# Putting the tail of the output product into the other arm of the range check's branch

## The chip, the cores and the metric

One core of a Trainium2 chip. The metric is the device time of one execution in microseconds (us), median of several; a few hundredths of a per cent matter here, so most readings are taken from the start times in the trace, which hold nanoseconds. PE is TensorE, PEld its weight loads, DVE is VectorE, ACT is ScalarE, POOL is GpSimd, SP is SyncE. A q behind an engine's name means its sequencer. "Product" means one matmul instruction; the operand that is loaded ahead of it is its weights, and it writes a PSUM tile, which VectorE's additions read. A run within 1.5% of the fastest run of its kernel is called fast.

## The reference

Attention of 8 x 32 queries over the last 2048 positions of a cache, 32 query heads on 4 key heads, with the projections ahead and behind:

```python
def reference(x, k_cache, v_cache, wq, wo):
    B, Sq, D = x.shape                      # 8, 32, 1024
    Hq, Dh = 32, 128
    Hkv, Sk = k_cache.shape[1], k_cache.shape[2]   # 4, 8192
    W = min(4096, max(256, Sk // 4))        # 2048
    ...
    scores = jnp.einsum("bhqd,bhkd->bhqk", q, k) * (Dh ** -0.5)
    p = _softmax(scores, axis=-1)
    o = jnp.einsum("bhqk,bhkd->bhqd", p, v)
    return (lambda x, *d: x.transpose(*d))(o, 0, 2, 1, 3).reshape(B, Sq, Hq * Dh) @ wo
```

## The kernel before

The kernel takes the exponentials without subtracting the row maximum, which is right while every row's sum stays in a range. It checks that range at the end, counts the rows that pass with a product against a column of ones, takes the minimum, and branches: if any row failed, an exact fallback runs instead (it never runs on this data). Every engine loads the flag into a register and branches. `hint_branch` puts a branch hint that names the fallback on PE's sequencer, 4.9 us ahead of the branch.

```python
            with tc.manual_schedule(engines=order):
                fast.run()
            hint_branch(tc, (E.PE,))
            with tc.manual_schedule(engines=order):
                flagi = fast.tail_begin()
        safe = nc.values_load(flagi[0:1, 0:1], min_val=0, max_val=1)

        with tc.If(safe < 1, label="fallback"):          # L78
            ...                                          # exact attention, exact output product
            out_proj(tc, wo, OT_e, out_flat, fast, ...)  # leaves state so that the tail gives the same result

        with tc.manual_schedule(engines=order):
            fast.tail_end()
```

The tail is the output product of the last key head for the last 128 rows. It has four column groups of 512, 256, 128 and 128 columns. Each group is eight products into one PSUM tile (a piece is two of them), one addition on VectorE and one output DMA. Before the change the 512-column group is issued ahead of the branch and everything else behind it:

```python
    def o_pieces(self, g, t, cuts=(512, 512)):
        ...
            if i == 0:
                st["ps"] = self.open_ps = self.ps_m.tile([P, 512], FP32, name="op_ps", tag="m")   # two buffers
            ps = st["ps"]
            for k in range(i * 2, i * 2 + 2) if mm is not False else ():
                nc.tensor.matmul(ps[:, 0:w], lhsT=self.OT[...], rhs=self.wo_t[gq][:, c, n0:n0 + w], ...)   # L293
            if i == 3 and mm is not True:
                ...
                    nc.vector.tensor_tensor(out=o_t[:, 0:w], in0=ps[:, 0:w], in1=acc, op=ALU.add)          # L303
                    eng = nc.sync if n0 in (0, 768) else nc.scalar
                    eng.dma_start(out=self.out[t * P:(t + 1) * P, n0:n0 + w], in_=o_t[:, 0:w])             # L305

    def tail_begin(self):
        self.pv_last()
        for p in self.after[:-2]:
            p()
        flagi = self.check_all()
        for p in self.after[-2:]:
            p()
        self.last = self.o_pieces(self.Hkv - 1, 1, (512, 256, 128, 128))
        for p in self.last[:3]:
            p()
        self.last[3](mm=True)
        return flagi

    def tail_end(self):
        self.last[3](mm=False)
        for p in self.last[4:]:
            p()

    def check_all(self):
        ...
        nc.tensor.matmul(cnt[0:1, 0:2 * ncol], lhsT=self.ones_c[:, :], rhs=self.ok[:, :, :], start=True, stop=True)   # L524, the count product
        low = ck.tile([1, 1], FP32, name="low")
        nc.vector.tensor_reduce(out=low[:, :], in_=cnt[0:1, 0:2 * ncol], op=ALU.min, axis=AX.X)                       # L526
        flagi = ck.tile([1, 1], I32, name="flagi")
        nc.vector.tensor_scalar(out=flagi[:, :], in0=low[:, :], scalar1=float(P) - 0.5, scalar2=None, op0=ALU.is_ge)  # L528
        return flagi
```

## Time and profile before

| | before |
|---|---|
| median of the first 3 runs | 187.18 us (186.95 to 484.08) |
| profiled run | 186.85 us, span 185.0 us, granted clock 1.0 |
| PE busy | 179.5 us, 97% of the span |
| start of the count product | 177.09 us |
| start of the last addition | 182.34 us |
| last output DMA issued / waited for by SP | 182.66 / 184.16 us |

The 484.08 us is the first of the runs and was not looked into. The distance from the start of the count product to the start of the last addition is called **the tail** from here on. Taken from the trace in nanoseconds it is 5.256 us. Everything the change touches lies in it.

In the timeline of the profile a line reads: start in us, length in us, engine, source line, operation, output tile <- input tiles, shapes, number of instructions merged, and in brackets how long the engine was idle before and what is thought to have ended that. First PE's products and then its weight loads, kernel before:

```profile
177.09 0.22 PE L524 MATMUL cnt_ps<-ok,ones_c 128*1 128x128 bf16 x1
177.24 2.76 PE L293 MATMUL op_ps<-wo_sb,OT 128*128 128x512 bf16 x12
180.15 2.15 PE L293 MATMUL op_ps<-wo_sb,OT 128*128 128x256 bf16 x24
...
177.96 1.54 PEld L293 LDWEIGHTS <-OT 128*128 128x128 bf16 x8 [0.19 <-DVE OT L422]
180.12 1.39 PEld L293 LDWEIGHTS <-OT 128*128 128x128 bf16 x17 [0.61 <-DVEq L78]
181.70 0.43 PEld L293 LDWEIGHTS <-OT 128*128 128x128 bf16 x7 [0.19 <-issue]
```

The second PE line is twelve products of 512 columns ahead of the branch, the third the 24 narrow ones behind it. Within a group the starts follow each other in 0.216 us (512 columns), 0.108 (256) and 0.056 (128); a product that keeps this distance is called in step. Across the branch they do not: the last product ahead of it starts at 179.620 and the next at 180.149, 0.529 later. 0.313 us are lost. The weight-load lines show both places where PE stood still: ahead of 180.12, and ahead of 181.70.

The events of the branch line on the sequencers of VectorE and PE, kernel before (operation, count, duration in ns min/median/max, start):

```profile
L78 DVEq COMPARE_BRANCH  x1: 72/72/72, 178.9 to 178.9; - x1
L78 PEldq COMPARE_BRANCH  x1: 249/249/249, 178.9 to 178.9; - x1
L78 DVEq EVENT_SEMAPHORE  x1: 21/21/21, 179.5 to 179.5; - x1
L78 PEldq EVENT_SEMAPHORE  x1: 51/51/51, 180.0 to 180.0; - x1
```

PE's sequencer runs ahead of its products: it branches at 178.9 while products issued earlier run until 180.0. But in the arm that is taken it then has a semaphore step, and that step happens only at 180.0. The arm is empty in the source. The build fills it, and as I read it because the fallback raises semaphores that the empty arm does not: an engine waits until its own count is complete and adds the difference. The label "DVEq L78" in the weight-load line names VectorE's step, which was long done at 179.5.

The VectorE lines of the same stretch, kernel before:

```profile
177.84 0.24 DVE L526 TENSOR_REDUCE low<-cnt_ps 1x1 f32<-1x128 f32 x1
178.11 0.14 DVE L528 TENSOR_SCALAR flagi<-low 1x1 int32<-1x1 f32 x1
180.04 0.69 DVE L303 TENSOR_TENSOR o_t<-op_ps,oacc 128x512 bf16<-128x512 f32 x1 [1.03 <-PE op_ps L293]
181.22 0.74 DVE L303 TENSOR_TENSOR o_t<-op_ps,oacc 128x256 bf16<-128x256 f32 x2 [0.49 <-PE op_ps L293]
182.34 0.29 DVE L303 TENSOR_TENSOR o_t<-op_ps,oacc 128x128 bf16<-128x128 f32 x1 [0.38 <-PE op_ps L293]
```

The fourth line merges two additions: the 256-column one (181.220 to 181.645) and the first 128-column one. The last group writes the PSUM buffer that the 256-column addition reads, and its first product starts at 181.697, right behind that addition's end; in step it would have been 181.466. That is a second loss of 0.231 us. The chain that ended last holds this wait (start, length, what):

```profile
181.22 0.43 DVE o_t L303
181.66 0.04 issue
181.70 0.62 PE op_ps L293 x8
```

### The profile page before, as it was taken

To read this page: it belongs to the slowest core of one execution; us is meant where nothing else is said; L and a number is where in the kernel's file an instruction comes from. 1 tells how busy PE (TensorE), PEld (TensorE's weight loads), DVE (VectorE), ACT (ScalarE), POOL (GpSimd) and SP (SyncE) were. 2 spreads that over 40 slices of the span, in tenths; PEclk is the share of its full clock that TensorE was granted. 3 is DMA by queue.
4 is the path that set the end of the run, shared out by engine and by line. 5 is a ranking of instruction groups with operands and counts; after the bars stand their busy time and mean duration, and the time that the engine had idled before them with its cause. 6 is when DMAs were issued, how large, how long until landed. Compare 5 with 4: busy or idle time off the path is not lost. (4 is left out here: it accounts for less than half of the span.)

```text
span 185.0 us, 5079 instructions
## 1 busy us (share of the span) xinstructions
PE 179.5 (97%) x2056; PEld 153.7 (83%) x2072; DVE 115.4 (62%) x268; ACT 131.8 (71%) x133; POOL 94.7 (51%) x150
## 2 busy tenths in 40 slices
PE   7999999999999999999999999999999999999993
PEld 2889999999999999987878999987777888888743
DVE  0138799994586685586467558647745855355372
ACT  2207899786789787878787677787877888888700
POOL 2000008949939959929944980796299289600000
PEclk9999999999999999999999999999999999999999
DMA  5999999998999999999999999999999999980012
GB/s 151 324 391 415 413 414 396 198 231 278 346 332 297 305 329 337 412 215 244 363 357 244 362 386 252 186 342 397 249 381 320 228 288 246 299 131 0 4 58 62
DMA packets 53082, 51.73 MB, mean 280 GB/s; under 512 B 39744, under 2 KB 40256, under 8 KB 53056
## 3 DMA queue, kind: packets, MB, share of 16 engines
q1 hardware_dynamic: 52480, 50.90, 97.8%
q10 hardware_dynamic: 576, 0.49, 0.8%
q8 instruction: 16, 0.26, 0.6%
q14 instruction: 10, 0.08, 0.1%
HBM read 41.42 MB, written 0.52 MB: 227 GB/s over the span
## 5 line engine op out<-in xcount | busy, mean ns | idle before, releaser
L469 ACT ACTIVATE pT<-s_ps 128x1024 bf16<-128x1024 f32 x128 | 128.9, 1025 | 33.3 <-PE s_ps L467 32.3
L259 POOL TENSOR_SCALAR kTv<-kb 32x512 bf16<-32x512 bf16 x140 | 93.7, 670 | 65.1 <-DMA k_raw<-in_k_cache_dram 26.7
L478 PEld LDWEIGHTS <-pT 128*128 128x128 bf16 x1024 | 68.5, 98 | 3.1
L467 PEld LDWEIGHTS <-kT 128*128 128x128 bf16 x368 | 34.8, 98 | 10.3
L293 PE MATMUL op_ps<-wo_sb,OT 128*128 128x512 bf16 (+2 forms) x128 | 33.0, 353 | 0.8
L273 PE MATMUL q_ps<-xT,wq_sb 128*128 128x256 bf16 x192 | 28.1, 273 | 0.0
L478 PE MATMUL o_ps<-va_112,pT 128*128 128x129 bf16 x352 | 27.1, 220 | 0.0
L478 PE MATMUL o_ps<-va_113,pT 128*128 128x129 bf16 x352 | 27.0, 220 | 0.1
L478 PE MATMUL o_ps<-va_114,pT 128*128 128x129 bf16 x320 | 24.7, 220 | 0.0
L249 DVE STREAM_TRANSPOSE kb<-k_raw 128x512 bf16<-128x512 bf16 x36 | 23.8, 684 | 0.0
L415 DVE RECIPROCAL RL_all<-o_ps 128x2 f32<-128x2 f32 x32 | 5.3, 164 | 27.5 <-PE o_ps L478 27.5
L420 DVE TENSOR_SCALAR o_sb<-o_ps,RL_all 128x128 bf16<-128x128 f32 x64 | 19.5, 346 | 1.1
L467 PEld LDWEIGHTS <-kTv 128*128 128x128 bf16 x144 | 13.9, 98 | 5.1
L273 PEld LDWEIGHTS <-wq_sb 128*128 128x128 bf16 x192 | 17.0, 98 | 1.2
L467 PE MATMUL s_ps<-QT_63,kT 128*128 128x256 bf16 x112 | 16.8, 273 | 0.0
L422 DVE STREAM_TRANSPOSE OT<-o_sb 128x256 bf16<-128x256 bf16 x32 | 14.3, 446 | 1.1
L467 PE MATMUL s_ps<-QT_66,kT 128*128 128x256 bf16 x96 | 14.4, 273 | 0.1
L293 PEld LDWEIGHTS <-OT 128*128 128x128 bf16 x144 | 11.3, 98 | 2.9 <-DVEq L78 0.6
L467 PE MATMUL s_ps<-QT_65,kT 128*128 128x256 bf16 x80 | 12.0, 273 | 0.1
L467 PE MATMUL s_ps<-QT_64,kT 128*128 128x256 bf16 x80 | 12.0, 272 | 0.1
L300 DVE TENSOR_TENSOR oacc<-op_ps,oacc 128x512 f32<-128x512 f32 x8 | 5.5, 683 | 7.4 <-PE op_ps L293 7.4
L409 DVE COPY va_113<-v_sb 128x2048 bf16<-128x2048 bf16 x11 | 9.5, 861 | 0.0
(46 smaller groups left out, 105.2 us busy)
## 6 DMA issues: line engine op xcount, KB each, us to landing
v_sb<-in_v_cache_dram SPq DMA_DIRECT2D x29, 512.0 KB, 6.8
wo_sb<-in_wo_dram SPq DMA_DIRECT2D x16, 512.0 KB, 6.8
wq_sb<-in_wq_dram SPq DMA_DIRECT2D x14, 512.0 KB, 7.4
k_raw<-in_k_cache_dram SPq DMA_DIRECT2D x13, 512.0 KB, 6.5
v_sb<-in_v_cache_dram SPq DMA_DIRECT2D x6, 256.0 KB, 5.8
wq_sb<-in_wq_dram SPq DMA_DIRECT2D x4, 256.0 KB, 6.4
kT<-in_k_cache_dram SPq DMA_TRANSPOSE x36, 6.6
k_raw<-in_k_cache_dram SPq DMA_DIRECT2D x2, 256.0 KB, 7.7
```

Of the source, the lines that this page charges most:

```text
L249: nc.vector.transpose(out=st["kb"][:, sl, :], in_=self.k_raw[ui][:, sl, :])
L259: nc.gpsimd.tensor_scalar(out=out, in0=in_, scalar1=1.0, scalar2=1.0, op0=ALU.mult, op1=ALU.mult)
L273: nc.tensor.matmul(st["ps"][:, 0:self.NQ], lhsT=self.wq_t[g, i][:, c % (DC // 2), hl * P:(hl + 1) * P], rhs=self.xT[:, c, :], start=(c == ...
L293: nc.tensor.matmul(ps[:, 0:w], lhsT=self.OT[:, gq, c, t * P:(t + 1) * P], rhs=self.wo_t[gq][:, c, n0:n0 + w], start=(k == 0), stop=(k == 7))
L300: nc.vector.tensor_tensor(out=acc, in0=ps[:, 0:w], in1=acc, op=ALU.add)
L409: self.nc.vector.tensor_copy(out=self.va[ui % 3][:, :, 0:self.Dh], in_=self.v_sb[ui][:, :, :])
L415: nc.vector.reciprocal(out=rl[:, ui * QT_N:(ui + 1) * QT_N], in_=o_ps[:, :, Dh])
L420: nc.vector.tensor_scalar(out=o_sb[:, qt, :, :], in0=o_ps[:, qt, 0:Dh].rearrange("p (i c) -> p c i", c=4), scalar1=rl[:, ui * QT_N + qt:ui ...
L422: nc.vector.transpose(out=self.OT[:, g * QT_N:(g + 1) * QT_N, :, b * self.Sq:(b + 1) * self.Sq], in_=o_sb[:, :, :, :])
L467: nc.tensor.matmul(s_ps[:, jj, :], lhsT=self.kT[ui][:, c * CJ + jj, :], rhs=q_u, start=True, stop=True)
L469: nc.scalar.activation(out=pT[:, :, :], in_=s_ps[:, :, :], func=ACT.Exp, bias=0.0, scale=self.scale)
L478: nc.tensor.matmul(o_ps[:, qt, 0:self.VW], lhsT=pT[:, jj, qt * P:(qt + 1) * P], rhs=va[:, j, 0:self.VW], start=(j == 0 and qt == 0), stop= ...
```

## The change

The intent: no wait at the branch. The tail becomes the other arm, so that the arm taken is not empty; the integer minimum is loaded directly, without a compare to a flag; the load stands eight products (four pieces) ahead of the branch; and the two 128-column groups take PSUM banks of another pool. That pool now lives longer, so the fallback gets by with less PSUM (its edits never run here, so no run shows that they are right).

```diff
@@ the branch
-                flagi = fast.tail_begin()
-        safe = nc.values_load(flagi[0:1, 0:1], min_val=0, max_val=1)
-
-        with tc.If(safe < 1, label="fallback"):
+                low = fast.tail_begin()
+                safe = nc.values_load(low[0:1, 0:1], min_val=0, max_val=P)
+                fast.tail_mid()
+
+        with tc.If(safe < P, label="fallback") as arms:
...
-        with tc.manual_schedule(engines=order):
-            fast.tail_end()
+        with arms.Else():
+            with tc.manual_schedule(engines=order):
+                fast.tail_end()
@@ pools
+        self.ps_o = pool("ps_o", 2, long_ctx, space=PSUM)
...
-        self.ps_o = pool("ps_o", 2, space=PSUM)
@@ o_pieces: the PSUM tile of a group may be handed in, in a dictionary st (parameter and call cut)
-            if i == 0:
-                st["ps"] = self.open_ps = self.ps_m.tile([P, 512], FP32, name="op_ps", tag="m")
-            ps = st["ps"]
+            if i == 0 and n0 not in st:
+                st[n0] = self.ps_m.tile([P, 512], FP32, name="op_ps", tag="m")
+            ps = st[n0]
@@ tail_begin (its lines self.open = {} and low = self.check_all() cut), tail_mid, tail_end
-        for p in self.last[:3]:
+        for p in self.last[:2]:
             p()
+        return low
+
+    def tail_mid(self):
+        self.last[2]()
         self.last[3](mm=True)
-        return flagi
+        for p in self.last[4:6]:
+            p()
+        for n0 in (768, 896):
+            self.open[n0] = self.ps_o.tile([self.P, 512], FP32, name="op_ps", tag="o_ps")
 
     def tail_end(self):
         self.last[3](mm=False)
-        for p in self.last[4:]:
+        for p in self.last[6:]:
             p()
@@ check_all
-        low = ck.tile([1, 1], FP32, name="low")
+        low = ck.tile([1, 1], I32, name="low")
         nc.vector.tensor_reduce(out=low[:, :], in_=cnt[0:1, 0:2 * ncol], op=ALU.min, axis=AX.X)
-        flagi = ck.tile([1, 1], I32, name="flagi")
-        nc.vector.tensor_scalar(out=flagi[:, :], in0=low[:, :], scalar1=float(P) - 0.5, scalar2=None, op0=ALU.is_ge)
-        return flagi
+        return low
@@ the fallback: scores copied to SBUF in pieces, the lines that prepared the shared tail removed (cut)
```

## The prediction

> **What bounds it now.** The page's first part has PE busy 97% of 185.0 us. Up to about 177 us the change alters no instruction's order on any engine. What counts is the tail, read from the timeline of the last 8 us: one 128x512 product every 0.216 us, the last one ahead of the branch starting at 179.62 and ending at 180.0. The chain that ended last then holds only PE products and VectorE additions, 180.15 to 182.63. The last output DMA is issued at 182.66, lands 1.5 us later, and 0.8 us of closing barriers follow.
>
> **What the tail loses before.** Two PE bubbles:
> 1. Branch, 0.31 us. The flag (142 ns on VectorE, after the 236 ns minimum) is ready at 178.25; PE's sequencer loads it from 178.29 to 178.78 and branches at 178.95 (0.25 us), while products queued ahead keep PE going. But the empty arm evens out semaphore counts: there PE's sequencer waits for PE's own last product (its step is at 180.04). The next product starts at 180.149 instead of 179.62+0.216=179.836. (PE's weight load shows 0.6 us idle, released by VectorE at L78; VectorE's step there was done by 179.55, so that label is not the cause.)
> 2. Buffer, 0.23 us. The last 128-column group reuses the PSUM buffer of the 256-column group and waits for its addition (ends 181.645): first product 181.697 instead of 181.410+0.056.
>
> **What the change does.** It removes the flag's compare, loads the integer minimum directly, eight products before the branch (four of 512, four of 256 columns), makes the tail the other arm (no self-wait of PE ahead of it), and gives the two 128-column groups the other pool's PSUM banks. The fallback's edits do not run.
>
> Walk: minimum ends 178.07, load about 178.11 to 178.60. Products queued ahead last until 178.97: no bubble expected, some 0.2 us to spare. Without the compare, the preceding 512-column addition ends near 178.8 instead of 179.0, so the 256 group's buffer is free in time. Branch about 179.2 to 179.45; the first product behind it is due at 179.836+4x0.108=180.27. The other engines need 0.46 to 0.59 us from branch start to their next instruction; even that fits. The Trainium skill ("Runtime: NRT & Kernel Launch", Instruction fetch mechanics) says that a taken branch outside the loaded window stalls for a fetch; the trace of before shows PE's own delay only as under 1.1 us. PE keeps its hint.
>
> So: last 256 product starts 180.59, addition 180.90 to 181.33; 128 groups back to back, additions from 181.35 and 181.80. The last addition started at 182.34 before: 0.54 us earlier. Landing and barriers follow unchanged; up to 0.1 may be lost as the last output DMAs come closer together. ScalarE gains a counting step behind its last issue, off the path.
>
> **Predicted.** 187.18 is the median of three with one outlier; the other runs are near 186.9. Saving about 0.5 us (0.3%): **186.6 us**, 8 in 10 between 186.1 and 187.2. Faster by over 2%: 0.01; within 2%: 0.98; slower: 0.01.
>
> **Right if** after shows no PE gap over 0.1 us between the count product and the last product; 256-column products every 0.108 us across the branch; the last group starting about 181.15 without waiting for VectorE; the last addition near 181.8; span near 184.5. **Wrong if** PE stalls at the earlier load (gap before the 512 products behind it) or behind the branch (fetch of the arm), or the last DMA takes longer to land.
>
> **What would make it wrong.** A 0.3 us stall of PE at load or branch cancels half; an arm on a page that is not loaded could cost 1 us; run-to-run scatter is about as large as the gain.

## More of the kernel before

The trace has PE's step as a wait for and a raise of one semaphore, 103, which PE's own products raise; the last of them raised it at 180.014, and the step starts at 180.042. So on PE the step waits for PE's own last product.

## The result, and the profile after

| | before | after |
|---|---|---|
| median | 186.95 us (186.69 to 484.08, 6 runs) | 186.38 us (185.89 to 187.06, 6 runs) |
| ratio of fast runs | | 0.9972, 95% interval 0.995 to 0.9995 |
| profiled span | 185.0 us | 184.6 us |
| start of the count product | 177.09 us | 177.14 us |
| tail | 5.256 us | 4.718 us |
| from the start of the last addition to the end of the span | 2.696 us | 2.695 us |

The ratio is the mean time of one kernel's fast runs over that of the other's of the same rounds, so it is not quite the ratio of the medians. By the interval it is a gain of 0.05 to 0.5%. The tail is 0.538 us shorter. The span is 0.48 us shorter, because the count product happened to start 0.06 us later in this profile.

PE's products and weight loads in the timeline, kernel after:

```profile
177.14 0.22 PE L534 MATMUL cnt_ps<-ok,ones_c 128*1 128x128 bf16 x1
177.29 4.53 PE L295 MATMUL op_ps<-wo_sb,OT 128*128 128x512 bf16 x36
...
178.02 3.63 PEld L295 LDWEIGHTS <-OT 128*128 128x128 bf16 x32 [0.19 <-DVE OT L424]
```

All 36 products are one line of 4.53 us now, and no start is over 0.011 us out of step. (One line alone would not show it: old_banks below has one of 36 products too, 4.76 us long, with two waits in it.) Both interruptions of the weight loads are gone. The events of the branch line, kernel after:

```profile
L79 DVEq COMPARE_BRANCH  x1: 72/72/72, 179.0 to 179.0; - x1
L79 PEldq COMPARE_BRANCH  x1: 263/263/263, 179.1 to 179.1; - x1
L79 POOLq EVENT_SEMAPHORE  x1: 17/17/17, 179.2 to 179.2; - x1
L79 ACTq EVENT_SEMAPHORE  x1: 17/17/17, 182.6 to 182.6; - x1
```

PE and VectorE have no semaphore step at the branch any more: the difference of the counts rides on their own products and additions (in the trace the arm's first product, at 180.328, raises PE's counter in the middle of its group). ScalarE has its step at 182.6, behind its last DMA issue, where nothing is held up by it. VectorE, kernel after:

```profile
177.89 0.24 DVE L536 TENSOR_REDUCE low<-cnt_ps 1x1 int32<-1x128 f32 x1
178.37 0.69 DVE L305 TENSOR_TENSOR o_t<-op_ps,oacc 128x512 bf16<-128x512 f32 x1 [0.24 <-PE op_ps L295]
180.16 1.54 DVE L305 TENSOR_TENSOR o_t<-op_ps,oacc 128x512 bf16<-128x512 f32 x3 [1.10 <-PE op_ps L295]
181.86 0.29 DVE L305 TENSOR_TENSOR o_t<-op_ps,oacc 128x128 bf16<-128x128 f32 x1 [0.15 <-PE op_ps L295]
```

The last addition waits 0.15 us for PE: the products bound the tail, and VectorE keeps up. The chain that ended last, followed back from the end, kernel after (start, length, what):

```profile
177.21 0.15 PE cnt_ps L534
177.36 4.48 PE op_ps L295 x36
181.84 0.02 issue
181.86 0.29 DVE o_t L305
```

### The profile page after: what moved, and what is told of

It reads as the page before. It is cut to its first block, busy times and chain, and to the rows that moved or that the text cites. A ratio compares the mean times of both kernels' runs of the same rounds, so it can differ in the third digit from the quotient of the medians.

```text
span 184.6 us, 5089 instructions
## 1 busy us (share of the span) xinstructions
PE 179.9 (97%) x2072; PEld 153.7 (83%) x2072; DVE 115.2 (62%) x267; ACT 131.8 (71%) x133; POOL 94.7 (51%) x150
## 4 chain that ended last, share of the span: by engine, by line
PE 93%; DMA 4%; SPq 1%; DVE 1%; issue 0%
PE o_ps L480 31%; PE s_ps L469 30%; PE op_ps L295 15%; PE q_ps L275 11%; DMA wq_sb<-in_wq_dram 4%; PE q_ps L377 2%; PE tp L236 2%; PE kf_ps L370 1%; SPq L164 0%; DVE kT L374 0%; SPq L321 0%; DVE o_t L305 0%; DVE QT_63 L397 0%; PE cnt_ps L534 0%
## 5 line engine op out<-in xcount | busy, mean ns | idle before, releaser
L295 PE MATMUL op_ps<-wo_sb,OT 128*128 128x512 bf16 (+2 forms) x144 | 36.2, 356 | 0.0
```

The lines of the kernel that those rows point to most:

```text
L295: nc.tensor.matmul(ps[:, 0:w], lhsT=self.OT[:, gq, c, t * P:(t + 1) * P], rhs=self.wo_t[gq][:, c, n0:n0 + w], start=(k == 0), stop=(k == 7))
```

## The experiments

The theory: the gain is the sum of two separate waits of PE. One is the empty arm's wait for PE's own last product (0.31 us), the other the shared PSUM buffer (0.23 us). The early load and the removed compare gain nothing. Rivals: all comes from one of the two; or the branch itself was slow and the eight products between load and branch hide it.

All kernels gave correct results. "Tail" is read from each run's profile; its scatter between three profiles of the changed kernel is 0.001 us. Times are given beside it where they were taken in rounds; the kernel before, on the same chips, had medians of 186.92, 186.85 and 186.82 us in the three sets of runs.

| kernel | tail, us | time, us | ratio to before (95%) |
|---|---|---|---|
| before | 5.256 | 186.95 | |
| after | 4.718 | 186.38 | 0.9972 (0.995 to 0.9995) |
| after_again | 4.718 | 186.60 | 0.9985 (0.9969 to 1.0001) |
| after_third | 4.717 | 186.50 | 0.9994 (0.998 to 1.0009) |
| old_banks | 4.947 | 186.72 | 0.9992 (0.9977 to 1.0007) |
| banks_only | 5.028 | 186.60 | 0.9982 (0.9965 to 0.9998) |
| empty_arm | 5.028 | 186.81 | 1.0004 (0.9978 to 1.0031) |
| branch_at_load | 4.777 | 186.58, one run | |
| no_hint | 4.744 | 186.54, one run | |
| no_branch | 4.717 | 186.51 | 0.9979 (0.9966 to 0.9993) |
| late_load | 4.716 | 186.49, one run | |
| compare_kept | 4.718 | 185.84, one run | |

The times cannot order kernels that differ by 0.1 us; the tails can. compare_kept has the lowest time of the table and exactly the tail of the changed kernel: in its profile the count product started at 176.65 us, in those of the changed kernel at 177.05, 177.14 and 177.45.

### old_banks: the branch part alone

```diff
-        for n0 in (768, 896):
-            self.open[n0] = self.ps_o.tile([self.P, 512], FP32, name="op_ps", tag="o_ps")
+        self.open[768], self.open[896] = self.open[0], self.open[512]
```

> The changed kernel, but the two 128-column groups write the PSUM tiles of the 512- and 256-column groups again and so wait for their additions. Tail = start of the count product to start of the last addition: 5.256 us before, 4.718 after. Theory (branch and buffer add up, 0.31 + 0.23): tail about 4.95, the last group's first product waiting for the 256-column addition some 0.2 us; time 0.2 to 0.3 us above the changed kernel. Rival (the whole gain comes from the branch): tail stays at 4.72 within 0.03. Rival (the whole gain comes from the buffers): tail 5.2 to 5.26.

Tail 4.947 us. Of the 0.538 us, 0.309 come without the new banks. The weight loads show one interruption, and none at the branch, kernel old_banks:

```profile
178.09 2.74 PEld L295 LDWEIGHTS <-OT 128*128 128x128 bf16 x17 [0.18 <-DVE OT L424]
180.99 0.97 PEld L295 LDWEIGHTS <-OT 128*128 128x128 bf16 x15 [0.15 <-issue]
```

One expectation was coarse: the wait is split. The first 128-column group waits for the 512-column addition (its first product 0.252 us behind the one ahead, instead of 0.109) and the last one for the 256-column addition (0.150 instead of 0.056). In the kernel before, the loss at the branch had hidden the first of these. The sum, 0.237, is what was expected.

### banks_only: the buffer part alone

The kernel before, with the pool, `o_pieces` and fallback edits of the change, and:

```diff
         self.last[3](mm=True)
+        for n0 in (768, 896):
+            self.open[n0] = self.ps_o.tile([self.P, 512], FP32, name="op_ps", tag="o_ps")
         return flagi
```

> The kernel before with only the two 128-column groups moved to the other pool's banks (and the fallback edit that makes room); branch, flag and empty arm as before. Theory: the 0.31 us gap ahead of the first 256-column product stays, the 0.23 us gap ahead of the last group goes: tail about 5.03. Rival (all from the branch): 5.25. Rival (all from the buffers): 4.72.

Tail 5.028 us: 0.228 us gained, and the first 256-column product is still 0.529 us behind the product ahead of it. The weight loads show this one interruption and no other, kernel banks_only:

```profile
178.10 1.54 PEld L293 LDWEIGHTS <-OT 128*128 128x128 bf16 x8 [0.19 <-DVE OT L422]
180.26 1.78 PEld L293 LDWEIGHTS <-OT 128*128 128x128 bf16 x24 [0.61 <-DVEq L78]
```

0.309 + 0.228 = 0.537, against 0.538 for the whole change. The two parts are separate and add up.

### empty_arm: everything but the filled arm

```diff
-        with tc.If(safe < P, label="fallback") as arms:
+        with tc.If(safe < P, label="fallback"):
...
-        with arms.Else():
-            with tc.manual_schedule(engines=order):
-                fast.tail_end()
+        with tc.manual_schedule(engines=order):
+            fast.tail_end()
```

(and the lines that let the fallback share the tail are back.)

> The changed kernel with its early integer load, its eight products between load and branch and its new banks, but the tail behind the If again, so that the arm taken is empty. Theory (the bubble is the empty arm's wait of PE for its own last product): the gap moves to the fifth 256-column product and is again about 0.3 us (start to start about 0.42 instead of 0.108); tail about 5.0. Rival (the bubble was the short distance from load to branch, and the products put between cure it): no gap over 0.1 us, tail about 4.72.

Tail 5.028 us, and the gap has moved with the branch: the fifth 256-column product starts 0.422 us behind the fourth, instead of 0.108. PE's weight loads and its step at the branch line, kernel empty_arm:

```profile
178.17 2.19 PEld L294 LDWEIGHTS <-OT 128*128 128x128 bf16 x12 [0.19 <-DVE OT L423]
180.76 1.34 PEld L294 LDWEIGHTS <-OT 128*128 128x128 bf16 x20 [0.40 <-issue]
```

```profile
L79 PEldq COMPARE_BRANCH  x1: 253/253/253, 179.3 to 179.3; - x1
L79 DVEq EVENT_SEMAPHORE  x1: 21/21/21, 179.7 to 179.7; - x1
L79 PEldq EVENT_SEMAPHORE  x1: 51/51/51, 180.7 to 180.7; - x1
```

The early load and the eight products between load and branch are all there, and the loss is back in full (0.314 us). PE branches at 179.3 and steps at 180.7, right behind its fourth 256-column product. VectorE's step is a full microsecond earlier. So the rival with the distance falls, and so does VectorE as a cause.

### after_again and after_third: the changed kernel beside the others

> The changed kernel once more, for its scatter beside the others: tail 4.72 within 0.03, time 0.4 to 0.6 us below before.

> The changed kernel beside check_later on the same chip: tail 4.72 within 0.03 from the count product, 5.73 within 0.03 from the last attention product; time about 0.5 us below before.

Tails 4.718 and 4.717 us; 5.73 us from the last attention product, as expected of after_third. The times gained less than expected: 0.9985 and 0.9994, where 0.54 us would be 0.9971. Taking all fast runs of all sets together, the changed kernel's 18 have a mean of 186.54 us and the 36 of before 186.87. The difference is 0.33 us; from the scatter of the single runs (0.30 and 0.24 us) its 95% interval is about 0.16 to 0.49, and the 0.54 us of the tail lie just outside it. Whether the part ahead of the tail runs some 0.2 us longer in the changed kernel, or the sample is only unlucky, the runs do not settle: of the kernel before there is one profile.

### branch_at_load and no_hint: what the distance and the hint buy

```diff
                 safe = nc.values_load(low[0:1, 0:1], min_val=0, max_val=P)
-                fast.tail_mid()
...
         with arms.Else():
             with tc.manual_schedule(engines=order):
+                fast.tail_mid()
                 fast.tail_end()
```

and for no_hint also

```diff
-            hint_branch(tc, (E.PE,))
```

> The changed kernel with the branch straight behind the early load, so that all eight products that stood between are in the arm. It shows what the distance buys: PE's products queued ahead end their run 1.89 us after the count product's start; the load ends at 1.52, the branch at about 1.95. Theory (the distance is needed, since the branch and its first instruction are not free): the fifth-from-last 512-column product comes late, by 0.1 us if PE's first instruction follows its branch at once, by 0.4 to 0.6 if PE's branch takes as long as on the other engines (0.46 to 0.59 from its start); tail 4.85 to 5.3. Rival (the distance is idle care, only the arm counts): tail 4.72 within 0.03.

> As branch_at_load, and PE's branch hint taken away. If the hint fetches the arm's code ahead: the gap at the branch grows, by 0.3 us or more. If the hint does nothing here (the fallback is the side it names, or the arm's page is loaded anyway): the same gap within 0.03 us.

Both missed. The tail of branch_at_load is 4.777 us, 0.06 above the changed kernel and below my range. PE's weight loads and branch, kernel branch_at_load:

```profile
178.18 0.68 PEld L295 LDWEIGHTS <-OT 128*128 128x128 bf16 x4 [0.18 <-DVE OT L424]
179.24 2.63 PEld L295 LDWEIGHTS <-OT 128*128 128x128 bf16 x28 [0.38 <-issue]
```

```profile
L78 PEldq COMPARE_BRANCH  x1: 253/253/253, 178.9 to 178.9; - x1
L78 DVEq COMPARE_BRANCH  x1: 72/72/72, 179.2 to 179.2; - x1
```

In the trace the branch runs from 178.927 to 179.180 and the first weight load of the arm starts at 179.236, 0.056 us later. So PE shows next to no delay behind its branch here. With the hint taken away the tail is 4.744 us: shorter, because the branch took 0.223 us instead of 0.253. By these two profiles, one of each kernel, the hint costs 0.03 us and helps nothing; in the changed kernel, whose tail is that of no_branch below, the distance hides that.

This answers a point that the prediction left open. The Trainium skill ("Runtime: NRT & Kernel Launch", Instruction fetch mechanics) warns of a stall on a taken branch whose target is not in the loaded window, and gives PE four times the instruction memory of most engines. The trace does not contradict it: in branch_at_load PE needs 0.31 us from the start of its branch to the next instruction, the 0.253 us of the branch and 0.056 us more, while in the kernel before VectorE, GpSimd, SP and ScalarE needed 0.46 to 0.59 us although their branch itself takes 0.045 to 0.072. That the rest is fetching is not shown.

### no_branch, late_load and compare_kept: what is left, and what was not needed

no_branch removes the If, the load, the hint and the fallback (the check is then without effect; the result is right on this data). late_load swaps two lines; compare_kept puts the flag back (with it the bound 1 of load and If, cut here):

```diff
-                safe = nc.values_load(low[0:1, 0:1], min_val=0, max_val=P)
                 fast.tail_mid()
+                safe = nc.values_load(low[0:1, 0:1], min_val=0, max_val=P)
```

```diff
-        low = ck.tile([1, 1], I32, name="low")
+        low = ck.tile([1, 1], FP32, name="low")
         ...
-        return low
+        flagi = ck.tile([1, 1], I32, name="flagi")
+        nc.vector.tensor_scalar(out=flagi[:, :], in0=low[:, :], scalar1=float(P) - 0.5, scalar2=None, op0=ALU.is_ge)
+        return flagi
```

> The changed kernel without the branch, the load and the fallback (right for this data, as no row fails the check; the minimum is still computed): the floor. Theory (after the change the branch costs PE nothing): tail 4.72 within 0.03, time within 0.2 us of the changed kernel. Rival (load or branch still cost somewhere): tail below 4.6 or time 0.3 us or more lower.

> The changed kernel with the load moved behind the eight products, right ahead of the branch. PE's sequencer passes the wait for the 256-column buffer at about 1.92 us after the count product's start, loads until about 2.45, branches until about 2.85; its next product is due at 3.186. Theory (the early load is spare): no gap if the first instruction follows within 0.3 us of the branch's end, tail 4.72; a gap of at most 0.3 otherwise, tail up to 5.0.

> The changed kernel with the compare to a flag (142 ns of VectorE) put back between the minimum and the early load. PE's load then runs from 1.20 to 1.69 us after the count product's start, and its next product, due at 1.89, is queued in time. Theory (the direct integer minimum gains nothing on the path): tail 4.72 within 0.03. Rival (the load is now so early that the compare is on the path): tail 4.80 to 4.90, with a gap at the fifth 512-column product of the last row of tiles.

Tails 4.717, 4.716 and 4.718 us. After the change the branch costs the tail nothing at all, so no better arrangement of the branch can shorten it. Neither the early load nor the integer minimum is on the path: in late_load the load runs from 1.97 to 2.46 us behind the start of the count product, PE branches until 2.82, and the next product, due at 3.19, is on time. A few hundredths are gained behind the tail in no_branch (2.662 us from the last addition to the end, instead of 2.69).

### check_later and count_later: a try to go lower

The count product costs PE more than the 0.056 us that a 128-column product takes in step: 0.308 us from the 512-column product ahead of it (0.216 in step) and 0.149 to the next, so 0.241 us in all. The profile puts the idle time of its weight load down to VectorE's range compares. So I moved the compares behind the transpose and the count behind eight products:

```diff
-        if ui == len(self.units) - 1:
-            self.check_units(ui, ui + 1)
         o_sb = ...
         nc.vector.transpose(...)
-        if ui == len(self.units) - 2:
-            self.check_units(0, ui + 1)
+        if ui >= len(self.units) - 2:
+            self.check_units(0 if ui < len(self.units) - 1 else ui, ui + 1)
@@ tail_begin (count_later: this hunk only; both also have late_load's edit)
-        low = self.check_all()
         ...
-        return low
+        return self.check_all()
```

> A try to go below the changed kernel: the load right ahead of the branch, the last unit's two range compares moved behind its transpose on VectorE, the count product moved behind eight of the output products on PE. Measured from the start of the last attention product to the start of the last addition (5.73 us after the change): the 0.09 us wait of PE for the compares and the 0.09 us restart behind the count go: 5.55 expected, if the branch, now about 0.6 us later, still hides behind the queued products. If it does not, 5.6 to 5.9. Time 0.1 to 0.2 us below the changed kernel, which the scatter of the times may hide.

> As check_later, but the two range compares stay ahead of the transpose. The fifth product behind the attention then waits for the transpose, which ends as late as before: 5.64 to 5.70 from the last attention product to the last addition, with a gap of 0.1 to 0.2 us ahead of the fifth product. If it is as short as check_later (5.55), the compares' place does not matter.

Both missed. From the last attention product to the last addition, check_later needs 5.951 us and count_later 5.958 us, against 5.73 of the changed kernel; check_later's time is 186.90 us, ratio 1.001 (0.9998 to 1.0022), beside 186.50 of after_third. PE's weight loads, kernel check_later:

```profile
178.99 0.08 PEld L531 LDWEIGHTS <-ones_c 128*1 128x1 bf16 x1 [0.42 <-DVE o_t L305]
179.14 1.20 PEld L295 LDWEIGHTS <-OT 128*128 128x128 bf16 x8
180.66 0.61 PEld L295 LDWEIGHTS <-OT 128*128 128x128 bf16 x7 [0.33 <-issue]
```

Compare the first line with the count's weight load after the change:

```profile
177.14 0.08 PEld L534 LDWEIGHTS <-ones_c 128*1 128x1 bf16 x1 [0.42 <-DVE ok L527]
```

The idle time is the same 0.42 us although the compares were done 0.92 us ahead of it this time (0.16 us in the changed kernel), and the pair of products around the count is again 0.458 us apart (0.242 more than in step). So my reading was wrong: the count did not wait for the compares. count_later settles it: there the count's weight load carries no wait for VectorE at all, and its idle time is 0.42 us again. It has a fixed cost that moves with it. What makes it so is open; it is the only product with a single column of weights, and its weights, and those of the product behind it, are loaded 2 to 4 ns ahead of their products and not during the product before. An experiment with 128 columns of ones would tell, and was not run. One more thing sets it apart: in every kernel it carries a wait for PE's own counter, semaphore 103, which the product ahead of it raises in the middle of its group. That wait is not shown to be the cost either: the raise is recorded 0.084 us after the count has started.

Of the 0.22 us that check_later lost up to the last addition, 0.21 are the branch, now too late. Its five loads of the minimum start within 0.012 us of each other and take 0.664 to 0.686 us, where they took 0.465 to 0.544 in the changed kernel. PE's branch then starts at 180.350, after its last queued product has started (180.344), and the next product comes 0.320 us later instead of 0.109: the "0.33 <-issue" of the third line. count_later lost 0.10 us there and 0.11 at the fifth product, which waited for the transpose, as expected. Its time, of one run, is 186.32 us.

The 0.22 us are about half of the 0.40 us by which check_later is slower than after_third. The other half lies behind the last addition: 2.879 us to the end of the span instead of 2.691. The last four output DMAs are issued within 0.84 us (1.30 in the changed kernel) and land 0.19 to 0.20 us apart, the last one 1.66 us after its issue; in the changed kernel it is 1.48. count_later shows the same spacing (2.837 us from the last addition to the end). That the closer issues are the cause was not tested.

## Why the prediction was right

- **Branch bubble, 0.31 us, cause and size: right.** old_banks shows 0.309 without the banks; empty_arm brings 0.314 back with all else in place, and PE's step follows its own last product in both kernels with an empty arm.
- **Buffer bubble, 0.23 us: right.** banks_only shows 0.228 alone, and the parts add up.
- **Walk through the tail: right to 0.01 us** once the 0.056 us later start of the count product is taken off: last group's first product at 181.16 (181.15 predicted), additions of the last three groups at 180.91, 181.36 and 181.80 (180.90, 181.35, 181.80). PE's branch came 0.14 us earlier than in the walk (179.06 instead of about 179.2), which cost nothing.
- **Removed compare and early load are off the path: right** (compare_kept, late_load).
- **One step was wrong.** "Without the compare, the preceding 512-column addition ends near 178.8 instead of 179.0": it ended at 179.06, or 179.00 with the later start taken off. It starts when PE's eighth product behind the attention is done (178.37, idle 0.24 us until then), so removing the compare only made VectorE wait. The buffer was free in time all the same.
- **The allowance of up to 0.1 us for DMAs coming closer together was not needed:** 2.696 and 2.695 us from the last addition's start to the end. (check_later, above, did lose 0.19 us there.)
- **The time:** 186.38 us lies in the range, near 186.6. The steady part, the tail, is shown to 0.001 us. How much of it the median shows depends on the part ahead of it, whose start of the tail varies by several tenths, and over all runs the measured gain is 0.33 us. That the first set's medians differ by 0.57 us, as the tail says, is partly luck: in the two later sets they differ by 0.32.

## What to carry to other kernels

An If without an Else is not free in the arm that does nothing: where the build evens out semaphore counts there, each engine has a step that waits, and PE's waited for its own last product (0.31 us here; the other engines' steps held up nothing). Putting the work that follows into the other arm removed PE's step without changing the order of its products. In a tail of tenths of microseconds, read the gaps between starts in the trace rather than the times, and distrust the name in a releaser label until moving that releaser moves the gap.

## What the Trainium skill lacked or had wrong

- "Advanced Engine Details and Errata", Control Flow Timing, gives about 108 ns for a compare-and-branch. Here it took 45 to 72 ns on four engines, and on PE 249 to 263 ns with a hint ahead, 223 without (one run).
- "TensorE: Matmul & The Clock Gate", Back-to-back issue gap, gives about 81 ns for sustained pairs of weight load and 128-column product and 131 ns for 512 columns. In this tail they follow each other in 0.055 to 0.057 us and in 0.216 us, with a new weight load for each; that is what the page gives for the isolated product.
- The same page, Architectural detail, says that PE can pull weight loads ahead of running products. That holds along the tail, where a weight load starts 1 to 2 ns behind the start of the product before its own, but not around the product with one column of weights, which costs 0.24 us beside neighbours of 0.216. No page that I read gives this cost, and its cause is open.
- No page that I read says that an arm without work can make an engine wait for its own instructions (0.31 us of PE here).
- "Runtime: NRT & Kernel Launch" tells of `TENSOR_LOAD` as a load from HBM, about 1.3 us in the preamble, and gives about 200 ns per register. A load of one integer that VectorE has just written, another kind of load, took 0.465 to 0.546 us with one to four engines at once, and 0.55 to 0.69 us with all five at once.
